# Norm statistics from sums and squares, a planner with measured step lengths, and two early gradient blocks in a forward-and-backward kernel of four layers

## The chip, the cores and the metric

The kernel runs on one NeuronCore of a Trainium2 chip. The metric is the time of one execution on the device in microseconds (us). Some executions of a program are slower as a whole. A profile is one execution taken with the hardware profiler. PE is TensorE (PEld its weight loads), DVE is VectorE, ACT is ScalarE, POOL is GpSimd. The granted clock is the share of PE's full clock that the profile shows as granted to it. An eviction is the copy of a matmul result out of PE's output memory.

## The reference

A residual stack of a linear-attention block A and a gated block B is applied twice (A, B, A, B; layers 0 to 3). Each block reads a layer norm without gain or bias. The kernel returns the result and all gradients.

```python
def _layernorm(x, axis=-1, eps=1e-5):
    m = jnp.mean(x, axis=axis, keepdims=True)
    v = jnp.var(x, axis=axis, keepdims=True)
    return (x - m) / jnp.sqrt(v + eps)
# x is (1, 2048, 512) bf16; A: 32 heads of 16; B: sigmoid(x @ w_gate) * (x @ w_up) @ w_down, width 1376
x = x + _A_ref(_layernorm(x), A_wqkv, A_wo)
x = x + _B_ref(_layernorm(x), B_w_gate, B_w_up, B_w_down)
x = x + _A_ref(_layernorm(x), A_wqkv, A_wo)
x = x + _B_ref(_layernorm(x), B_w_gate, B_w_up, B_w_down)
# outputs: x, and the gradients of A_x, A_wqkv, A_wo, w_gate, w_up, w_down for a given grad_out
```

## The kernel before

The tokens are worked in 8 blocks of 256, each in two halves of 128, in five sweeps over the blocks; the weight gradients end the program. The order of all instructions comes from a small planner in the kernel. Each piece of work states how long it holds PE (`pe`), which steps follow on other engines and how long each takes (`post`), and which buffers it takes and gives back. While the program is built, an event loop plays these pieces through. Whenever an engine is idle, the ready piece with the longest remaining path is emitted on it. The emitted order is then fixed: an engine runs its instructions in that order, whatever the real times are.

```python
class Plan:
    HOP = dict(PE=0.22, A=0.16, V=0.16, P=0.16, D=2.2)   # us from the end of a step to its follower
    SLACK = 1.3                                          # stretches the paths that set priorities
    RATE = 0.27                                          # MB per us of a DMA
    ...
EARLY = 1
PULL = (10.0, 10.0, 0.0)          # extra priority of some transposes
AHEAD2, AHEAD3 = (2, 0), (2, 0)   # how far attention may run ahead of the gated block
TURN = (0, 1, 1)                  # which blocks are transposed by PE and which by DMA
```

The norm of half a block takes its statistics on DVE:

```python
nc.vector.bn_stats(stats[:], x_t[:, j, :])
nc.vector.bn_aggr(mv[:], stats[:])
nc.gpsimd.tensor_scalar(rs, mv[:, 1:2], EPS_LN, None, ALU.add)
nc.gpsimd.tensor_tensor(rs, rs, k.neghalf[:, 0:1], ALU.pow)
nc.vector.scalar_tensor_tensor(nmr[:], mv[:, 0:1], -1.0, rs, ALU.mult, ALU.mult)
nc.scalar.activation(h[:, j, :], x_t[:, j, :], ACT.Identity, bias=nmr[:], scale=rs)
...
# in a_p2, the residual add of a linear-attention block:
nc.vector.tensor_tensor(k.x[l, b][:, j, :], ps[:], st["xin"][:, j, :], ALU.add)
```

In the last gated layer, `EARLY` says for how many blocks the product of the output gradient with the transposed down weights (`dhh`) is made ahead, as pieces of its own. It depends only on inputs, so it can fill holes.

Of the kernel before, what the change touches and what calls it, by code (L numbers as in the profile page):

```python
# [17 lines left out]
D = 512  # L18
# [56 lines left out]
class Plan:  # L75
# [8 lines left out]
    HOP = dict(PE=0.22, A=0.16, V=0.16, P=0.16, D=2.2)  # L84
    SLACK = 1.3
# [5 lines left out]
    def add(self, key, fn, pe=0.0, deps=(), post=(), use="", side=False, pull=0.0):  # L91
        u = Piece(len(self.pieces), key, fn, pe, list(deps), [(p + ("",))[:3] for p in post], marks(use), side, pull)
        u.post = [(e, c, marks(m)) for e, c, m in u.post]
        assert key not in self.by_key, key
        self.pieces.append(u)
        self.by_key[key] = u
# [168 lines left out]
PHI = [("A", 0.5, "+s1"), ("V", 0.2), ("V", 0.62, "-s1 -mm")]  # L265
EARLY = 1
PULL = (10.0, 10.0, 0.0)
AHEAD2, AHEAD3 = (2, 0), (2, 0)
TURN = (0, 1, 1)
# [126 lines left out]
def build_consts(k, consts):  # L396
    nc = k.nc
    k.consts = consts
    k.ident = consts.tile([P, P], BF16, name="ident")
    nc.gpsimd.memset(k.ident[:], 0.0)  # L400
    nc.gpsimd.affine_select(out=k.ident[:], in_=k.ident[:], compare_op=ALU.not_equal, fill=1.0,
                            base=0, pattern=[[-1, P]], channel_multiplier=1)
    k.neghalf = consts.tile([P, 2], F32, name="neghalf")
    nc.gpsimd.memset(k.neghalf[:], -0.5)
    k.ones_col = consts.tile([P, 1], BF16, name="ones_col")
    nc.gpsimd.memset(k.ones_col[:], 1.0)
    k.bdmask = consts.tile([P, P], BF16, name="bdmask")
    nc.gpsimd.memset(k.bdmask[:], 1.0)
    nc.gpsimd.affine_select(out=k.bdmask[:], in_=k.bdmask[:], compare_op=ALU.is_ge, fill=0.0,
                            base=0, pattern=[[-16, 8], [0, 16]], channel_multiplier=1)  # L410
    nc.gpsimd.affine_select(out=k.bdmask[:], in_=k.bdmask[:], compare_op=ALU.is_ge, fill=0.0,
                            base=15, pattern=[[16, 8], [0, 16]], channel_multiplier=-1)

    k.hs = consts.tile([P, NDC, P], BF16, name="hs")
    nc.gpsimd.memset(k.hs[:], 0.0)
    for o in (0, H):
        v = k.hs[:, :, o:o + H]
        nc.gpsimd.memset(v, 1.0)
        nc.gpsimd.affine_select(out=v, in_=v, compare_op=ALU.is_ge, fill=0.0,
                                base=0, pattern=[[128, NDC], [-16, H]], channel_multiplier=1)  # L420
        nc.gpsimd.affine_select(out=v, in_=v, compare_op=ALU.is_ge, fill=0.0,
                                base=15, pattern=[[-128, NDC], [16, H]], channel_multiplier=-1)
    k.spread = consts.tile([P, NDC, P], BF16, name="spread")
    k.rr = [consts.tile([P, 2, P], BF16, name=f"rr{i}") for i in range(2)]
    for r in k.rr:
        nc.gpsimd.memset(r[:], 0.0)
    k.rr_i = 0
    k.rstd = [consts.tile([P, 2 * NBLK], F32, name=f"rstd{l}") for l in range(4)]
    k.rstdh = {l: consts.tile([P, 2 * NBLK], F32, name=f"rstdh{l}") for l in (1, 3)}
# [25 lines left out]
def add_turn(k, key, get, put, name, deps, pull=0.0):  # L455
# [8 lines left out]
    for j in range(2):  # L464
        k.G.add(f"{key}.{j}", lambda j=j: half(j), NDC * C128, deps[j] + ([f"<{key}.0"] if j else []), [("A", 0.52, "-tp")],
                "+tp" if j else "+tp +t2", pull=pull)
# [12 lines left out]
def layernorm(k, l, b, x_fn, deps):  # L479

    nc, G = k.nc, k.G

    def half(j):
# [19 lines left out]
        if l in k.rstdh:  # L503
            yield
            nc.gpsimd.tensor_scalar(k.rstdh[l][:, col], rs, 0.5, 0.0, ALU.mult, ALU.add)
    for j in range(2):
        G.add(f"LN{l}.{b}.{j}", lambda j=j: half(j), 0.0, deps[j] + ([f"LN{l}.{b}.0@s"] if j else []),
              [("V", 0.62, "+ln @s"), ("V", 0.07), ("P", 0.19), ("P", 0.63), ("V", 0.07), ("A", 0.7, "@h" if l in k.rstdh else "@h -ln")]
              + ([("P", 0.25, "-ln")] if l in k.rstdh else []), "" if j else "+t2")
# [16 lines left out]
def a_k(k, l, b, keep, by_dma=False):  # L526
# [69 lines left out]
    if l == 2 and b in SUMS:  # L596
        gs, prev = SUMS[b]
        for m in range(NDC):
            G.add(f"GS{n}.{m}", lambda m=m: gsum(m, gs, True, True), 2 * len(gs) * C512,
                  [f"K{l}.{bb}.{j}" for bb in gs for j in range(2)] + [f"GS{l}.{prev}.{m}"] + ([f"<GS{n}.{m - 1}"] if m else []),  # L600
                  [("A", 0.5, "-mm") if b == 1 else ("V", 0.62, "-mm")],
                  "+mm" + (" +accf" if b == 1 and m == 0 else " +w4" if b == NBLK - 1 and m == 0 else ""))
    if b % 2 == 1:
        bs = [b - 1, b]
        ks = [f"K{l}.{bb}.{j}" for bb in bs for j in range(2)]
        G.add(f"ZS{n}", zsum, 16 * 0.027, ks + [f"ZS{l}.{b - 2}", f"ZB{l - 2}"], [("V", 0.1, "-tp")], "+tp")
# [13 lines left out]
def cpost(i, tag):  # L620
    return [("A", 0.5, "-" + tag)] if i % 2 == 0 else [("V", 0.6, "-" + tag)]


def a_barrier(k, l):
# [42 lines left out]
    G.add(f"KV{l}", kv, 16 * C128, cg + ["WV", f"KT{l - 2}", f"WT{l - 2}.3", f"ZN{l - 2}"], [("V", 0.62, "-mm")], "+mm")  # L667
# [33 lines left out]
    for m in range(NDC):  # L701
        G.add(f"WT{l}.{m}", lambda m=m: wpt(m), 4 * C128, wps + ([f"<WT{l}.{m - 1}"] if m else []), [("A", 0.5, "-mm")],
              "+mm" if m else "+mm +w4")
    if l == 0:
        G.store("SW", lambda: nc.sync.dma_start(out=k.WpT_d[:], in_=flat(A.WpT[:])), 2 * BLK, [f"WT{l}.{m}" for m in range(NDC)], "-w4")
    G.add(f"ZB{l}", zbd, 0.0, [f"ZS{l}.{last}"] + wps, [("V", 0.7, "+s1"), ("V", 0.1)])
    G.add(f"ZN{l}", lambda: turn("Zn"), 4 * C128, [f"ZB{l}"], [("A", 0.5, "-tp")], "+tp -s1")
    G.add(f"KT{l}", lambda: turn("kv"), 4 * C128, wps, [("A", 0.5, "-tp")], "+tp")
# [32 lines left out]
def a_p2(k, l, b, xin_fn, deps, late):  # L741
# [54 lines left out]
    def y(j):  # L796
# [3 lines left out]
        for c in range(NDC):  # L800
            nc.tensor.matmul(ps[:], lhsT=A.pn[b][:, c, tslice(j)], rhs=A.Wp[:, c, :], start=(c == 0), stop=(c == NDC - 1))  # L801
        yield
        nc.vector.tensor_tensor(k.x[l, b][:, j, :], ps[:], st["xin"][:, j, :], ALU.add)
    G.load("LX" + n, lx, BLK if l == 0 else 2 * BLK, [f"YA{l}.{b - 2}.1", f"SX{l - 1}.{b}"] + deps, "+t2" if l == 0 else "+xb")
    G.add("DE" + n, den, 8 * 0.027, [f"Q{n}.0", f"Q{n}.1", f"ZZ{l}", f"<YA{l}.{b - 2}.1"],
          [("V", 0.15, "+dn -tp"), ("V", 0.5), ("V", 0.1, "+rr"), ("V", 0.12, "-dn")], "+tp")
    G.add("RT" + n, turn, 2 * C128, ["DE" + n, "SPREAD"] + late, [("V", 0.3, "-tp +rT")], "+tp -rr")
    for hf in range(2):
        G.add(f"SP{n}.{hf}", lambda hf=hf: spread(hf), 2 * C256, ["RT" + n] + ([f"<SP{n}.0"] if hf else []),
              [("V", 0.62, "@pn"), ("V", 0.2, "+s1"), ("V", 0.62, "-s1 -mm")], "+mm" if hf else "+mm +t2 +t2")  # L810
# [8 lines left out]
    for j in range(2):  # L819
        G.add(f"YA{n}.{j}", lambda j=j: y(j), 4 * C512, pn + ["LX" + n] + [f"WP{l}.{c}" for c in range(NDC)] + ([f"<YA{n}.0"] if j else []),  # L820
              [("V", 0.62, "-mm")], "+mm +xb" if j == 0 and l == 0 else "+mm")
# [4 lines left out]
def a_b1(k, l, b, deps):  # L826
# [56 lines left out]
    for j in range(2):  # L883
        G.add(f"CA{n}.{j}", lambda j=j: cast(j), 0.0, [f"LB{lx}.{b}.{j}", "LN_" + n, f"<MS{l}.{b - 2 if b % 2 else b - 3}.3"]
              + ([f"CA{n}.0"] if j else []), [("A", 0.52)], "" if j else "+t2")
    add_turn(k, f"TG{n}", lambda: st["g"], lambda t: st.__setitem__("gT", t), f"gT{l}", [[f"CA{n}.{j}"] for j in range(2)])
    for hf in range(2):
        G.add(f"DP{n}.{hf}", lambda hf=hf: dpn(hf), 8 * C256,
              [f"TG{n}.0", f"TG{n}.1"] + ([f"LP{n}", "WPL0"] if l == 0 else [f"LP{n}"]) + ([f"<DP{n}.0"] if hf else [f"<DP{l}.{b - 1}.1"]) + [f"WT{l}.{m}" for m in range(NDC)],
              [("V", 0.45), ("V", 0.45)], "+mm +s1" if hf else "+mm +s1 +t2")  # L890
        G.add(f"ZE{n}.{hf}", lambda hf=hf: zn(hf), 2 * C256, [f"DP{n}.{hf}", f"ZN{l}"] + ([f"<ZE{n}.0"] if hf else [f"<ZE{l}.{b - 1}.1"]),
              [("V", 0.45), ("V", 0.45, "-s1"), ("V", 0.6, "-mm")], "+s1 -s1")
# [3 lines left out]
    if b in SUMS:  # L896
# [20 lines left out]
        for m in range(NDC):  # L917
# [3 lines left out]
                  [("A", 0.5, "-mm") if b == 1 else ("V", 0.62, "-mm")],  # L921
# [4 lines left out]
def a_bbarrier(k, l):  # L926
# [61 lines left out]
    G.add(f"DT{l}", dkvT, 16 * C128, ms + ["WOT"], [("V", 0.62, "-mm")], "+mm +s1")  # L988
# [3 lines left out]
    G.add(f"DZ{l}", dz, 0.0, [f"ZE{l}.{b}.{hf}" for b in range(NBLK) for hf in range(2)], [("V", 0.12)] * 5)  # L992
# [3 lines left out]
    G.add(f"DKV{l}", dkv, 16 * C128, [f"<U{l}.3"] + ms, [("V", 0.62, "-mm")], "+mm")  # L996
# [23 lines left out]
def add_lnb(k, l, b, fn, deps, ps_tag, more=""):  # L1020

    for j in range(2):
        k.G.add(f"LB{l}.{b}.{j}", lambda j=j: ln_bwd(k, l, b, j, *fn(j)), 0.0, deps[j] + ([f"LB{l}.{b}.0@s"] if j else []),
                [("A", 0.7, "@s +lnf +s1 -" + ps_tag), ("V", 0.66, "-s1"), ("P", 0.3), ("V", 0.62), ("V", 0.65, "-lnf")],
# [3 lines left out]
def a_b2(k, l, b, x_load, out, deps, out_use=""):  # L1028
# [51 lines left out]
    for hf in range(2):  # L1080
        G.add(f"DK{n}.{hf}", lambda hf=hf: half(hf), 8 * C256, ["LDH" + n, "LDP" + n, f"DZ{l}"] + ([f"<DK{n}.0"] if hf else [f"<DK{l}.{b - 1}.1"]) + [f"U{l}.{m}" for m in range(NDC)],
              [("V", 0.2, "+s1"), ("V", 0.4), ("V", 0.4, "-s1 -mm")], "+mm" if hf else "+mm +t2")
# [11 lines left out]


# [30 lines left out]
def glu_fwd(k, l, b):  # L1126
# [28 lines left out]
    def y(p):  # L1155
# [6 lines left out]
        if p == NPAIR - 1:  # L1162
            for j in range(2):
                yield
                nc.vector.scalar_tensor_tensor(x[0, b][:, j, :], st["acc"][j][:], 0.5, x[0, b][:, j, :], ALU.mult, ALU.add)
    for p in range(NPAIR):
# [3 lines left out]
              [("A", 0.46, "+th -mm"), ("V", 0.58, "-mm @hh"), ("P", 0.55), ("V", 0.58, "-th")],  # L1170
              "+mm +mm" if p else "+mm +mm +hh +w11")
        G.add(f"Y{n}.{p}", lambda p=p: y(p), q * 2 * C512, [f"G{n}.{p}@hh", "WD"] + ([f"<Y{n}.{p - 1}"] if p else []),
              [("V", 0.62, "-acc @0"), ("V", 0.62, "-acc")] if p == NPAIR - 1 else [], "" if p else "+acc +acc")
# [37 lines left out]
def glu_both(k, l, b):  # L1211
# [58 lines left out]
    if early:  # L1270
        for p in range(NPAIR):
            G.add(f"E{n}.{p}", lambda p=p: dhh_early(p), len(pair_chunks(p)) * 4 * C256,
                  ["LG" + n, "WWD"] + ([f"<E{n}.{p - 1}"] if p else [f"<E{l}.{b - 1}.5"]), [("A", 0.46, "-mm")],
# [4 lines left out]
    for p in range(NPAIR):  # L1278
        q = len(pair_chunks(p))
        ops = [("A", 0.46, "+th -mm"), ("A", 0.46, "+s1 +s1 +pr -mm"), ("V", 0.58, "-mm @hh"), ("V", 0.58, "@u"), ("V", 0.58, "-th"), ("V", 0.35, "-s1 -s1")]  # L1280
        mm = "+mm +mm +mm"
        if early:
            ops = [ops[0], ("V", 0.58, "+s1 +pr -mm @hh")] + ops[3:5] + [("V", 0.35, "-s1")]
# [3 lines left out]
              ops, mm if p else mm + " +hh")  # L1287
# [23 lines left out]
    for j in range(2):  # L1311
        G.add(f"Y3{n}.{j}", lambda j=j: part(j), 11 * C512, [f"G{n}.{p}@hh" for p in range(NPAIR)] + ([f"<Y3{n}.0"] if j else []),
              [("V", 0.62, "-mm")], "+mm" if j else "+mm +t2")
# [6 lines left out]
def glu_bwd(k, l, b):  # L1320
# [43 lines left out]
    for j in range(2):  # L1364
        G.add(f"CB{n}.{j}", lambda j=j: cast(j), 0.0, [f"LB2.{b}.{j}"] + ([f"CB{n}.0"] if j else []), [("A", 0.52)],
              "" if j else "+th" if b < 2 else "+hh" if b in (2, 4) else "+t2" if b > 5 else "")
    add_turn(k, "TB" + n, lambda: k.g1[b], lambda t: st.__setitem__("gT", t), "gT1", [[f"CB{n}.{j}", f"<G1{l}.{b - 1}.1"] for j in range(2)], PULL[2])
    for p in range(NPAIR):
# [3 lines left out]
              [("A", 0.46, "+s1 +pr -mm"), ("V", 0.35, "@u"), ("V", 0.35, "-s1")], "+mm")  # L1372
# [85 lines left out]
def sweep2(k):  # L1458
# [10 lines left out]
    for b in range(NBLK):  # L1469
        a_p2(k, 0, b, lambda b=b: xin(b), [f"LN2.{b - 3}.1@h", f"<G1.{b - AHEAD2[0]}.0"], [f"<G1.{b - AHEAD2[0]}.{AHEAD2[1]}"])  # L1470
        layernorm(k, 1, b, lambda b=b: k.x[0, b], [[f"YA0.{b}.{j}"] for j in range(2)])
# [7 lines left out]
        layernorm(k, 2, b, lambda b=b: k.x[0, b], [[f"Y1.{b}.5@0", f"<GS2.{2 * (b // 2) - 3}.3"], [f"Y1.{b}.5"]])  # L1479
        G.free("-xb", [f"LN2.{b}.{j}" for j in range(2)] + [f"SX1.{b}"])  # L1480
        a_k(k, 2, b, b < 2, TURN[0] <= b < last)
# [5 lines left out]
def sweep3(k):  # L1487
# [19 lines left out]
    for b in range(NBLK):  # L1507
        a_p2(k, 2, b, lambda b=b: xin(b), [f"<Y33.{b - 3}.1", f"<G3.{b - AHEAD3[0]}.0"], [f"<G3.{b - AHEAD3[0]}.{AHEAD3[1]}"])
        layernorm(k, 3, b, lambda b=b: k.x[2, b], [[f"YA2.{b}.{j}"] for j in range(2)])
# [67 lines left out]
def dw(k):  # L1577
# [60 lines left out]
    def epost(i):  # L1638
        return [("A" if i % 2 == 0 else "V", 0.6, "+s1 -mm")]
# [94 lines left out]
    mid = [f"<J{ng[0] - 4}.3"]  # L1734
    for m in range(NDC):
        G.add(f"JV.{m}", lambda m=m: dwv(m), 8 * C128, ["FG0", "FG2", "DKV0", "DKV2"] + mid, epost(m), "+mm")
        G.store(f"SV.{m}", lambda m=m: nc.sync.dma_start(out=k.outs["wqkv"][cslice(m), 2 * D:3 * D], in_=st["v", m][:]), BLK / 2, [f"JV.{m}"], "-s1")
        G.add(f"JO.{m}", lambda m=m: dwo(m), 2 * C512, ["FM0", "FM2"] + mid, epost(m + 1), "+mm")
# [31 lines left out]
```

## Time and profile before

The median was 1141.45 us in three runs (1141.18 to 1143.3).

The page of the profile of the kernel before: the span, then busy time, share of the span and number of instructions by engine.

```profile
span 1137.5 us, 20073 instructions
PE 1089.5 (96%) x7652; PEld 711.2 (63%) x7652; DVE 694.7 (61%) x1711; ACT 337.5 (30%) x639; POOL 119.9 (11%) x295
```

PE is the bound. Since no matmul can be dropped, what is to be won is PE's idle time, 1137.5 − 1089.5 = 48.0 us, and a little more where PE runs at a lower clock. The next view shows where the idle time is. These are windows of the same execution: the window and its length, then busy time and instruction count of PE, PEld, DVE, ACT and POOL, and at the end the granted PE clock, the share of the DMA engines and GB/s.

```profile
0.00:50.00 50.00, 41.34 (x313) 23.95 (x314) 34.39 (x98) 34.58 (x57) 16.77 (x52) 1.00 0.78 250
50.00:90.00 40.00, 33.18 (x291) 24.75 (x290) 35.42 (x90) 17.14 (x29) 7.84 (x18) 0.96 0.35 109
...
205.00:290.00 85.00, 74.23 (x616) 50.57 (x614) 71.48 (x161) 31.90 (x55) 12.22 (x29) 1.00 0.83 197
290.00:520.00 230.00, 227.95 (x1632) 154.68 (x1630) 180.50 (x422) 81.23 (x154) 20.94 (x49) 1.00 0.70 180
520.00:610.00 90.00, 84.10 (x553) 51.02 (x552) 66.79 (x181) 27.15 (x56) 2.29 (x9) 0.98 0.81 230
...
740.00:870.00 130.00, 121.26 (x720) 67.77 (x718) 94.48 (x258) 29.52 (x66) 4.74 (x20) 0.99 1.03 246
870.00:1140.00 270.00, 262.75 (x1839) 178.43 (x1836) 19.05 (x35) 15.06 (x32) 0.00 (x0) 1.00 0.89 195
```

The length less PE's busy time is PE's idle time: 8.7, 6.8, 10.8, 2.0, 5.9 and 8.7 us, and to the end of the span 4.8 us (267.5 − 262.75). The holes lie where one sweep gives way to the next (50-90, 205-290, 520-610, 740-870) and at both ends. In between PE is full, even in 90-205, where DVE is 91% busy (104.57 of 115 us).

What PE waited for, longest in total first (engine and tile, releaser, total us, times, longest), whole execution:

```profile
PE hTk_ps L450 <- ACT h L502: 7.0, 1, 7.0
PE ya_ps L801 <- DVE rphiT L794: 3.6, 3, 2.3
PE dpn_ps L857 <- DVE dqT L880: 2.9, 2, 2.5
PE q_ps L726 <- DMA hTq<-h_d: 2.3, 1, 2.3
```

The first is the start of the program. The rest are many small waits, none over 2.5 us.

The statistics on DVE, as groups of instructions (line, engine, operation, tiles, shapes, count, then busy us and mean ns of one, then idle time of the engine before them):

```profile
L492 DVE BATCH_NORM_STATS2 ln_stats<-xa 128x6 f32<-128x512 f32 x32 | 21.5, 671 | 0.0
L494 DVE BATCH_NORM_AGGREGATE ln_mv<-ln_stats 128x2 f32<-128x6 f32 x64 | 11.0, 172 | 0.3
L500 DVE SCALAR_TENSOR_TENSOR ln_nmr<-ln_mv,rstd 128x1 f32<-128x1 f32 x64 | 11.0, 172 | 4.1 <-POOL rstd L498 3.9
```

### The profile page before, as it was taken

To read this page: it belongs to the slowest core of one execution; us is meant where nothing else is said; L and a number is where in the kernel's file an instruction comes from. 1 tells how busy PE (TensorE), PEld (TensorE's weight loads), DVE (VectorE), ACT (ScalarE), POOL (GpSimd) and SP (SyncE) were. 2 spreads that over 40 slices of the span, in tenths; PEclk is the share of its full clock that TensorE was granted. 3 is DMA by queue.
4 is the path that set the end of the run, shared out by engine and by line. 5 is a ranking of instruction groups with operands and counts; after the bars stand their busy time and mean duration, and the time that the engine had idled before them with its cause. 6 is when DMAs were issued, how large, how long until landed. Compare 5 with 4: busy or idle time off the path is not lost.

```text
span 1137.5 us, 20073 instructions
## 1 busy us (share of the span) xinstructions
PE 1089.5 (96%) x7652; PEld 711.2 (63%) x7652; DVE 694.7 (61%) x1711; ACT 337.5 (30%) x639; POOL 119.9 (11%) x295
## 2 busy tenths in 40 slices
PE   7979999978999999999899999997999999999998
PEld 4657666646566676676555665654544456666787
DVE  6789989779867987778956577678754000000001
ACT  7642444334333333234144444431211000000001
POOL 4123435201201000100000000000000000000000
PEclk9999999999999999999999999999999999999999
DMA  7737898994777767755979979979999999999852
GB/s 240 244 93 242 237 297 227 262 217 131 199 192 187 185 172 190 189 164 150 249 206 284 252 216 270 271 188 255 283 250 261 245 229 234 201 281 216 148 115 70
DMA packets 491392, 242.97 MB, mean 214 GB/s; under 512 B 297280, under 2 KB 475680, under 8 KB 489248
## 3 DMA queue, kind: packets, MB, share of 16 engines
q1 hardware_dynamic: 491296, 241.69, 83.0%
q8 instruction: 60, 0.98, 0.4%
q14 instruction: 36, 0.29, 0.1%
HBM read 68.75 MB, written 100.43 MB: 149 GB/s over the span
## 4 chain that ended last, share of the span: by engine, by line
PE 86%; DVE 6%; DMA 3%; ACT 2%; issue 2%; SPq 1%; POOL 0%; DVEq 0%; ACTq 0%
PE dw_ps L1652 25%; PE dha_ps L1072 7%; PE dh_acc L1186 7%; PE dh_acc L1188 7%; PE dhh_ps L1119 6%; PE g_ps L1119 6%; PE u_ps L1119 6%; PE y_ps L1307 3%; PE y_acc L1160 3%; PE dpk_ps L1056 2%; PE ya_ps L801 2%; PE k_ps L537 2%; PE dpn_ps L857 2%; PE m_ps L906 2%; PE g_ps L563 2%
## 5 line engine op out<-in xcount | busy, mean ns | idle before, releaser
L1652 PE MATMUL dw_ps<-dw_set,h 128*128 128x352 bf16 (+2 forms) x1536 | 205.6, 297 | 0.0
L1652 PEld LDWEIGHTS <-h 128*128 128x128 bf16 x1536 | 150.3, 98 | 55.1
L1635 DVE TENSOR_SCALAR dw_o<-dw_ps 128x512 bf16<-128x512 f32 (+3 forms) x33 | 17.8, 541 | 246.6 <-PE dw_ps L1652 242.0
L1186 PE MATMUL dh_acc<-wuT,du 128*128 128x512 bf16 x352 | 133.4, 379 | 1.2 <-ACT lnb_t L1007 1.2
L1188 PE MATMUL dh_acc<-wgT,dg 128*128 128x512 bf16 x352 | 133.4, 379 | 0.2 <-DVE dg L1361 0.2
L1633 ACT ACTIVATE dw_o<-dw_ps 128x512 bf16<-128x512 f32 (+4 forms) x34 | 16.3, 481 | 264.7 <-PE dw_ps L1652 249.2
L1119 PE MATMUL g_ps<-hT,wg 128*128 128x256 bf16 x704 | 92.5, 272 | 0.1
L1119 PE MATMUL u_ps<-hT,wu 128*128 128x256 bf16 x704 | 92.5, 273 | 0.0
L1119 PE MATMUL dhh_ps<-gT,wdT 128*128 128x256 bf16 x704 | 89.7, 273 | 1.1 <-ACT dhh L1268 0.7
L1119 PEld LDWEIGHTS <-wg 128*128 128x128 bf16 x704 | 68.2, 98 | 20.4 <-issue 0.4
L1652 PE MATMUL dw_ps<-g,dw_set 128*128 128x512 bf16 (+1 forms) x352 | 78.4, 384 | 1.6 <-DVE dqT L880 1.6
L1119 PEld LDWEIGHTS <-wdT 128*128 128x128 bf16 x704 | 68.7, 98 | 15.7 <-issue 1.8
L1119 PEld LDWEIGHTS <-wu 128*128 128x128 bf16 x704 | 68.9, 98 | 8.0
L1013 POOL TENSOR_SCALAR ab<-c 128x2 f32<-128x2 f32 x64 | 18.8, 294 | 505.3 <-DVE lnb_j L1010 505.2
L1652 PEld LDWEIGHTS <-dw_set 128*128 128x128 bf16 (+1 forms) x352 | 35.5, 101 | 42.7 <-issue 3.7
L1188 PEld LDWEIGHTS <-dg 128*128 128x128 bf16 x352 | 34.4, 98 | 35.4 <-issue 1.5
L1186 PEld LDWEIGHTS <-du 128*128 128x128 bf16 x352 | 34.4, 98 | 33.1
L1241 ACT ACTIVATE th<-g_ps 128x512 f32<-128x512 f32 (+1 forms) x48 | 26.9, 559 | 91.5 <-PE g_ps L1119 63.5
L1007 ACT ACTIVATE lnb_t<-dha_ps,rstd 128x512 f32<-128x512 f32 x32 | 22.0, 687 | 88.3 <-PE dha_ps L1072 59.6
L1160 PE MATMUL y_acc<-wd,hh 128*128 128x512 bf16 x176 | 43.2, 379 | 0.0
L1359 DVE TENSOR_TENSOR du<-s2tl,dhh 128x512 bf16<-128x512 bf16 (+1 forms) x48 | 19.0, 400 | 39.3 <-ACT dhh L1354 36.4
L1144 ACT ACTIVATE th<-g_ps 128x512 f32<-128x512 f32 (+1 forms) x48 | 26.8, 557 | 54.6 <-PE g_ps L1119 32.8
(187 smaller groups left out, 1833.0 us busy)
## 6 DMA issues: line engine op xcount, KB each, us to landing
s2t_d<-s2t SPq DMA_DIRECT2D x8, 1408.0 KB, 6.8
s2tl<-s2t_d SPq DMA_DIRECT2D x8, 1408.0 KB, 8.1
hh_d<-hh SPq DMA_DIRECT2D x16, 640.0 KB, 4.5
du_d<-du SPq DMA_DIRECT2D x80, 128.0 KB, 2.8
dg_d<-dg SPq DMA_DIRECT2D x80, 128.0 KB, 2.7
h_d<-h SPq DMA_DIRECT2D x32, 256.0 KB, 2.7
h<-h_d SPq DMA_DIRECT2D x18, 256.0 KB, 4.5
pk_d<-pk SPq DMA_DIRECT2D x16, 256.0 KB, 3.1
```

The lines of the kernel that those rows point to most:

```text
L537: nc.tensor.matmul(ps[:], lhsT=A.hT[b][:, m, tslice(j)], rhs=k.wk[:, m, :], start=(m == 0), stop=(m == NDC - 1))
L563: nc.tensor.matmul(ps[:], lhsT=k.h[l, bb][:, j, cslice(m)], rhs=A.pk[bb][:, j, :], start=(first and i == 0), stop=(last and i == len(its) ...
L801: nc.tensor.matmul(ps[:], lhsT=A.pn[b][:, c, tslice(j)], rhs=A.Wp[:, c, :], start=(c == 0), stop=(c == NDC - 1))
L1072: nc.tensor.matmul(ps[:], lhsT=lh[:, c, tslice(j)], rhs=rh[:, c, :], start=(i + c == 0), stop=(i == 2 and c == NDC - 1))
L1119: nc.tensor.matmul(ps[:, i, :], lhsT=w[:, m, fsl(fc)], rhs=rhsT[:, m, :], start=(m == 0), stop=(m == NDC - 1))
L1144: nc.scalar.activation(th[:, 0:w], flat(gp[:])[:, 0:w], ACT.Tanh, scale=0.5)
L1160: nc.tensor.matmul(st["acc"][j][:], lhsT=st["hh"][:, fc, tslice(j)], rhs=k.wd[:, fc, :], start=(fc == 0), stop=(fc == NFC - 1))
L1186: nc.tensor.matmul(acc[j][:], lhsT=du[:, i, tslice(j)], rhs=k.wuT[:, fc, :], start=(fc == 0), stop=False)
L1188: nc.tensor.matmul(acc[j][:], lhsT=dg[:, i, tslice(j)], rhs=k.wgT[:, fc, :], start=False, stop=(fc == NFC - 1))
L1241: nc.scalar.activation(th[:, 0:w], flat(gp[:])[:, 0:w], ACT.Tanh, scale=0.5)
L1307: nc.tensor.matmul(ps[:], lhsT=st["hh"][:, fc, tslice(j)], rhs=k.wd[:, fc, :], start=(fc == 0), stop=(fc == NFC - 1))
L1652: nc.tensor.matmul(ps, lhsT=lhs(s_), rhs=rhs(s_), start=(s_ == 0), stop=(s_ == 31))
```

## The change

Its intent has three parts. First, 46 of the 64 norm halves take their statistics off DVE: the residual adds also sum their result, ACT sums the squares, and POOL does the small arithmetic. Second, the planner gets the step lengths that the trace shows, a `LAP` of 0.08 us by which a step overlaps the one before it on its engine, and a slack of 1. Third, two blocks instead of one make `dhh` early. With these go new settings and freer placement of the last small weight gradients (`JV`, `JO`). The diff, cut to its core (`...` marks cuts):

```diff
-    HOP = dict(PE=0.22, A=0.16, V=0.16, P=0.16, D=2.2)
-    SLACK = 1.3
+    HOP = dict(PE=0.25, A=0.14, V=0.14, P=0.14, D=2.2)
+    LAP = 0.08
+    SLACK = 1.0
...
-        u.post = [(e, c, marks(m)) for e, c, m in u.post]
+        u.post = [(e, c if e == "D" else c - self.LAP, marks(m)) for e, c, m in u.post]
...
-PHI = [("A", 0.5, "+s1"), ("V", 0.2), ("V", 0.62, "-s1 -mm")]
-EARLY = 1
-PULL = (10.0, 10.0, 0.0)
-AHEAD2, AHEAD3 = (2, 0), (2, 0)
-TURN = (0, 1, 1)
+PHI = [("A", 0.6, "+s1"), ("V", 0.29), ("V", 0.69, "-s1 -mm")]
+EARLY = 2
+SUMMED = (0, 7, 0)     # layer 1: blocks from 0; layer 2: blocks below 7; layer 3: blocks from 0
+PULL = (10.0, 10.0, 10.0)
+AHEAD2, AHEAD3 = (2, 3), (2, 0)
+TURN = (6, 1, 1)
...
+    def half_sums(j):
...
+        nc.scalar.activation(h[:, j, :], x_t[:, j, :], ACT.Square, accum_out=q[:, 0:1])
+        nc.gpsimd.tensor_tensor(q[:, 1:3], sx.to_broadcast([P, 2]), k.pm[:], ALU.mult)
+        nc.gpsimd.tensor_scalar(q[:, 0:1], q[:, 0:1], 1.0 / D, EPS_LN, ALU.mult, ALU.add)
+        nc.gpsimd.tensor_scalar(rs, q[:, 1:2], q[:, 2:3], q[:, 0:1], ALU.mult, ALU.add)
+        nc.gpsimd.tensor_tensor(rs, rs, k.neghalf[:, 0:1], ALU.pow)
+        nc.gpsimd.tensor_tensor(q[:, 3:4], q[:, 1:2], rs, ALU.mult)
+        nc.scalar.activation(h[:, j, :], x_t[:, j, :], ACT.Identity, bias=q[:, 3:4], scale=rs)
...
-        nc.vector.tensor_tensor(k.x[l, b][:, j, :], ps[:], st["xin"][:, j, :], ALU.add)
+        nc.vector.scalar_tensor_tensor(k.x[l, b][:, j, :], ps[:], 1.0, st["xin"][:, j, :], ALU.mult, ALU.add,
+                                       accum_out=k.sx[l + 1][:, 2 * b + j:2 * b + j + 1])
... (the same accum_out on the other residual add; some forty step lengths replaced)
-    mid = [f"<J{ng[0] - 4}.3"]
-        G.add(f"JV.{m}", lambda m=m: dwv(m), 8 * C128, ["FG0", "FG2", "DKV0", "DKV2"] + mid, epost(m), "+mm")
+        G.add(f"JV.{m}", lambda m=m: dwv(m), 8 * C128, ["FG0", "FG2", "DKV0", "DKV2"], epost(m), "+mm", pull=40.0)
```

## The prediction

> **What bounds the kernel now.** TensorE. The page gives PE 1089.5 us busy of a 1137.5 us span (96%); DVE 61%, ACT 30%, POOL 11%. The chain of waits is 86% PE. In the PE timeline back-to-back matmuls start 109 ns (256 columns) or 216 ns (512 columns) apart, so a busy PE is at its pace. Only PE idle time, about 48 us, can be won. Windows of 25 us place it: 0-25 has 7.8 us idle (7.0 of it before the first transpose), 50-75 6.3, 225-275 10.8, 300-325 1.5, 525-575 5.5, 750-800 7.3, 825-850 1.4, and about 5 us of tail, mostly the last store. 100-225 and 870-1130 are full. In 50-75, 525-550 and 775-800 the granted clock is 0.93: each loses some 1.7 us more. The Trainium skill ("TensorE: Matmul & The Clock Gate", Part 1) says an idle window of about 3.4 us halves the clock; the trace agrees that the clock falls only where the PE waits.
>
> **What the change removes, adds, moves.** No matmul goes, one more block (8 transposes, 0.4 us) is added.
> - DVE: 46 normalisation halves lose BN_STATS (671 ns), BN_AGGREGATE (172) and the -mean*rstd op (172): about 47 us. The adds that now also sum cost perhaps 0.05-0.1 us each, 48 of them: +3 us. Net about -43 us, 30 of it in 55-250.
> - ACT: 46 x (a square pass of about 0.69 plus a 0.2 accumulator read, the durations of the lnb_t pair) = +41 us.
> - POOL: four more 0.29 us scalar steps, less one, per half: +40 us. POOL has room, but the chain of one half becomes longer: 2.7 us before, about 3.5 after, without queueing.
> - Two early blocks instead of one: 4.8 us of dhh matmuls become free to fill the start of the third sweep, and one block is turned by PE, not DMA.
> - Schedule from measured step lengths. The gradient pieces of V and O move off the last microseconds.
>
> **How much is critical.** DVE is 92-98% busy in 100-200, but PE is full there, so relief there buys nothing at once. It helps at the edges, where PE waits name DVE:
> - 50-75 (waits on rphiT 3.6 us, pqT 1.7 us): I expect 2.5-3 us back plus part of the cold clock.
> - 225-275 (pk, z, Zn, h, the hTq load 2.3): 4-5 us, of which most by the second early block.
> - 525-575 and 750-850 have the same work on DVE; 1-2 us by better ordering.
> - 300-325 and tail: 1 us.
> DMA waits (hTq 2.3 us, hT 1.4, first load) stay.
> Sum: about 11 us.
>
> **Predicted: 1130 us, 8 in 10 between 1118 and 1140.** Faster by over 2% (below 1118.6): 0.10. Within 2%: 0.87. Slower by over 2%: 0.03.
>
> **What would show it.** PE busy within 3 us of 1089; PE idle down from 48 to about 37. Windows: idle in 50-75 near 3.5, in 225-275 near 6, in 750-800 still over 5. DVE busy about 650, ACT about 380, POOL about 160. Granted clock in 50-75 above 0.93. DVE share in 100-200 falls to 80%, PE there unchanged.
>
> **What would make it wrong.** The square leaving the table set of exp and tanh: more than the one ACT_TABLE_LOAD (1.28 us) of now ("ScalarE: Activation LUTs", Table sets, says a set holds a fixed group; no run here shows square in it). The longer POOL chain delaying the transposed blocks at the start of a sweep. The new order colliding with DMA, which is at 1.0 share in 200-250. Or a much better order at the two backward transitions, which I have not credited: that could win 8 us more.

## More of the kernel before

The transposed weights `wuT` and `wgT` are loaded by DMA, and a small memset on POOL then clears padding rows. The planner does not count this memset as a step.

## The result, and the profile after

The changed kernel took 1131.49 us (median of 4, 1127.41 to 1133.16), against 1142.38 us (4 runs, 1141.18 to 1144.55) for the kernel before. The ratio is 0.9897, with a 95% interval of 0.9865 to 0.9929. A ratio in this document is the mean time of one kernel's fast runs over that of the other's of the same rounds, so it is not quite the ratio of the medians quoted. Later the same changed kernel was run again as a control (label c0_after_again), on a chip where the kernel before took 1138.58 us: 1131.24 us, ratio 0.9932 (0.9919 to 0.9945). So the gain is 7 to 11 us, under one per cent to about one. The two ratios of one and the same kernel differ by 0.0035, which is 4 us: differences of that size between rounds say little.

The page of the changed kernel, and the engine line of the control:

```profile
span 1131.4 us, 20151 instructions
PE 1083.4 (96%) x7559; PEld 710.9 (63%) x7660; DVE 663.1 (59%) x1621; ACT 365.6 (32%) x733; POOL 156.1 (14%) x435
```

```profile
PE 1090.0 (96%) x7660; PEld 710.8 (63%) x7660; DVE 662.9 (59%) x1621; ACT 365.9 (32%) x733; POOL 156.8 (14%) x435
```

The first trace holds only 7559 matmul records for 7660 weight loads, so its PE busy time is too small. The control has all 7660, and PE's idle time is read from it: its span was 1130.6 us, so 1130.6 − 1090.0 = 40.6 us were idle, 7.4 less than before. The windows of the control:

```profile
0.00:50.00 50.00, 40.03 (x292) 22.19 (x293) 33.48 (x93) 33.37 (x55) 16.70 (x54) 1.00 0.79 247
50.00:90.00 40.00, 36.03 (x307) 26.28 (x305) 35.65 (x91) 17.74 (x35) 11.43 (x33) 0.96 0.35 105
...
205.00:290.00 85.00, 78.90 (x617) 51.82 (x616) 64.61 (x147) 39.11 (x76) 21.98 (x57) 0.98 0.86 211
290.00:520.00 230.00, 227.63 (x1650) 155.77 (x1648) 175.98 (x402) 87.17 (x175) 28.79 (x74) 1.00 0.71 180
520.00:610.00 90.00, 82.22 (x548) 49.29 (x547) 64.68 (x180) 28.25 (x59) 2.92 (x10) 1.00 0.80 221
...
740.00:870.00 130.00, 123.00 (x722) 68.28 (x721) 92.05 (x242) 28.09 (x63) 5.56 (x20) 0.99 1.05 251
870.00:1140.00 270.00, 257.67 (x1815) 176.14 (x1813) 17.41 (x33) 14.96 (x32) 0.00 (x0) 1.00 0.87 189
```

PE's idle time by stretch (its length, the last one cut at the end of the span, less PE busy); the last column is a kernel that comes up later:

| stretch, us | before | changed (control) | c1_searched |
|---|---|---|---|
| 0-50 | 8.7 | 10.0 | 9.7 |
| 50-90 | 6.8 | 4.0 | 4.1 |
| 90-205 | 0.3 | 0.0 | 0.0 |
| 205-290 | 10.8 | 6.1 | 1.4 |
| 290-520 | 2.0 | 2.4 | 2.1 |
| 520-610 | 5.9 | 7.8 | 3.7 |
| 610-740 | 0.0 | 0.5 | 0.0 |
| 740-870 | 8.7 | 7.0 | 7.1 |
| 870-end | 4.8 | 2.9 | 2.9 |
| all | 48.0 | 40.6 | 31.0 |

Three holes shrank (50-90, 205-290, the end) and one a little (740-870); two grew (0-50, 520-610). The longest waits of PE in the control read the same way: small, and still naming DVE and ACT.

```profile
PE hTk_ps L456 <- ACT h L532: 6.9, 1, 6.9
PE hTk_ps L456 <- ACT hTk L458: 4.0, 4, 2.0
PE ya_ps L833 <- DVE rphiT L826: 3.9, 2, 2.0
```

The groups of the changed kernel that replaced the statistics, and the only table load of ACT:

```profile
L496 ACT ACTIVATE h<-xa 128x512 bf16<-128x512 f32 x30 | 18.8, 626 | 25.5 <-DVE xa L835 19.4 <-DVE xa L1203 5.8
L496 ACT ACTIVATION_READ_ACCUMULATOR h<-xa 128x1 f32 x30 | 5.7, 189 | 0.0
L532 ACT ACT_TABLE_LOAD x1 | 1.3, 1283 | 3.7 <-DMA x<-in_A_x_dram 3.7
L835 DVE DVE_READ_ACCUMULATOR x2l<-ya_ps,x2l 128x1 f32 x16 | 1.4, 86 | 0.0
L502 POOL TENSOR_SCALAR rstd<-ln_q 128x1 f32<-128x1 f32 x46 | 21.4, 465 | 3.4
```

The summing add costs no more than the add (679 to 688 ns before and after); its sum is read out by an instruction of its own of 82 to 86 ns. The square takes 626 ns and its read-out 189 ns.

The end of the program also changed. The last pieces of the chain of waits of the kernel before (start, us, what), then of the changed kernel:

```profile
1130.94 2.81 DMA out_dram<-dw_o
1133.87 0.69 DVE dw_o L1635
```

```profile
1092.72 35.82 PE dw_ps L1691 x328
1128.61 0.38 ACT dw_o L1672
```

Before, the last pieces were eight short ones in a row (`JV`, `JO`), and the last eviction waited until a store had given an output buffer free. After, the end is one ordinary group and its eviction. That is the step from 4.8 to 2.9 us in the table.

### The profile page after: what moved, and what is told of

It is laid out like the page before. It is cut to its first block, busy times and chain, and to the rows that moved or that the text cites. A ratio compares the mean times of both kernels' runs of the same rounds, so it can differ in the third digit from the quotient of the medians.

```text
span 1131.4 us, 20151 instructions
## 1 busy us (share of the span) xinstructions
PE 1083.4 (96%) x7559; PEld 710.9 (63%) x7660; DVE 663.1 (59%) x1621; ACT 365.6 (32%) x733; POOL 156.1 (14%) x435
## 4 chain that ended last, share of the span: by engine, by line
PE 85%; DVE 6%; SPq 2%; ACT 2%; issue 2%; DMA 1%; POOL 1%; DVEq 0%; ACTq 0%
PE dw_ps L1691 24%; PE dha_ps L1105 7%; PE dh_acc L1227 7%; PE g_ps L1157 6%; PE u_ps L1157 6%; PE dhh_ps L1157 6%; PE dh_acc L1225 6%; PE y_ps L1346 3%; PE y_acc L1198 3%; PE q_ps L758 2%; PE dpk_ps L1089 2%; PE ya_ps L833 2%; PE k_ps L569 2%; PE m_ps L939 2%; PE g_ps L595 1%
## 5 line engine op out<-in xcount | busy, mean ns | idle before, releaser
L1225 PE MATMUL dh_acc<-wuT,du 128*128 128x512 bf16 x323 | 122.5, 379 | 0.3
L1280 ACT ACTIVATE th<-g_ps 128x512 f32<-128x512 f32 (+1 forms) x48 | 26.8, 558 | 55.3 <-PE g_ps L1157 42.1
L1187 DVE SCALAR_TENSOR_TENSOR hh<-th,u_ps 128x512 bf16<-128x512 f32 (+1 forms) x48 | 30.8, 641 | 18.5 <-ACT th L1182 11.4
```

The costliest lines, as they stand in the source:

```text
L1187: nc.vector.scalar_tensor_tensor(hh, th[:, 0:w], 1.0, flat(up[:])[:, 0:w], ALU.add, ALU.mult)
L1225: nc.tensor.matmul(acc[j][:], lhsT=du[:, i, tslice(j)], rhs=k.wuT[:, fc, :], start=(fc == 0), stop=False)
L1280: nc.scalar.activation(th[:, 0:w], flat(gp[:])[:, 0:w], ACT.Tanh, scale=0.5)
```

## The experiments

The question was which part gives the gain. Theories:

- **Edges**: the relief of DVE and the second early block fill the holes at the sweep starts. This is the prediction's reason.
- **Order**: the true step lengths, by themselves, make a better order.
- **Luck**: any new order moves the time by some us, up or down.
- **Planner** (formed after the first four runs): the settings had been chosen so that the planner's own end time is low. What moves that end time moves the time on the chip, and no part has a value of its own.

The planner's end time is called *planned* below. It is what the event loop in the kernel works out while the program is built. It is not a measurement. It is 1139.2 us for the kernel before (with its old lengths) and 1124.1 us for the changed one. All kernels here gave correct results. The first four kernels ran beside the kernel before at a median of 1138.73 us, the next four at 1138.58 us, the last four at 1138.92 us; each of these rounds was on another chip, so ratios are compared across them, not times.

### First: the change less one part

`a1_no_sums`: all statistics back on DVE.

```diff
-SUMMED = (0, 7, 0)
+SUMMED = (8, 0, 8)
... (and the two residual adds without accum_out)
```

> The changed kernel with the norm statistics put back on VectorE (all 64 halves by BN_STATS, the residual adds without sums); everything else of the change kept. Edges theory (relief of VectorE and the early block fill the two sweep starts): 3 to 5 us slower than the changed kernel, ratio to the kernel before about 0.993, the loss in 50-90 us; 205-290 us keeps its gain. Order theory (the step lengths make the better order): within 1.5 us of the changed kernel, ratio 0.989 to 0.991. Luck theory (any new order moves the time by some us, up or down): change of either sign, in stages that the statistics do not touch as well.

Measured: 1142.29 us, ratio 1.0028 (1.0009 to 1.0047). That is 0.0096, or 11 us, worse than the control's ratio: more than the whole gain of the change. PE idle in 50-90 rose to 6.2 us, as expected. But the loss is not there alone: in 205-290 PE idled *less* (3.7 us) than in the changed kernel.

`a2_one_early`: one early block.

```diff
-EARLY = 2
+EARLY = 1
```

> The changed kernel with one early gradient block instead of two. Edges theory: 3 to 4 us slower than the changed kernel, ratio about 0.993, with the lost PE time of 205-290 us back from 8.7 to about 12.5 us and 50-90 us still near 5.7. Order theory: within 1.5 us of the changed kernel. Luck theory: either sign, elsewhere too.

Measured: 1136.28 us, ratio 0.9967 (0.9948 to 0.9986), 4 us worse than the control. The size fits the edges theory. The place does not. These are the windows 205-290 and 290-520 of the changed kernel's first trace and then of this one (both traces lack 100 or 101 matmul records, so they can be compared with each other):

```profile
205.00:290.00 85.00, 77.53 (x604) 51.58 (x612) 64.31 (x146) 38.77 (x75) 21.88 (x57) 0.98 0.85 210
290.00:520.00 230.00, 226.00 (x1621) 155.78 (x1648) 176.05 (x402) 87.12 (x175) 28.73 (x74) 1.00 0.71 180
```

```profile
205.00:290.00 85.00, 78.96 (x615) 52.62 (x623) 65.39 (x150) 38.95 (x77) 21.81 (x57) 0.98 0.84 217
290.00:520.00 230.00, 220.16 (x1580) 151.70 (x1605) 173.65 (x408) 86.60 (x173) 25.55 (x74) 1.00 0.67 174
```

Without the second early block PE is busier in 205-290 (78.96 against 77.53 us) and idler in 290-520 (9.8 against 4.0 us). So the second block did not fill the hole at the start of the third sweep. One reason can be read from the traces: of the second block's 44 `dhh` matmuls the changed kernel placed few there. It ran 60 `dhh` matmuls in 205-290 (the kernel before 44, this one 52), and 16 more at 0.109 us are 1.7 us. The loss came later: most of it lies in 440-480, where PE idled 6.1 us here and 0.3 us in the changed kernel. Whether the missing block or the new order did that is not shown.

`a3_old_steps`: the old step lengths, hops and slack; everything else as changed.

```diff
-    HOP = dict(PE=0.25, A=0.14, V=0.14, P=0.14, D=2.2)
-    LAP = 0.08
-    SLACK = 1.0
+    HOP = dict(PE=0.22, A=0.16, V=0.16, P=0.16, D=2.2)
+    SLACK = 1.3
... (all step lengths as before)
```

> The changed kernel ordered with the old step lengths (old hops, no overlap term, slack 1.3, old costs); statistics, early blocks, turns and ends as in the change. Edges theory: within 2 us of the changed kernel, ratio 0.988 to 0.992. Order theory: 5 us or more slower, ratio 0.995 to 1.0, the loss spread over all sweep changes. Luck theory: either sign, a few us.

Measured: 1153.91 us, ratio 1.0126 (1.0103 to 1.0150), 22 us worse than the control. This favours the order theory, or luck.

`a4_old_knobs`: the old settings and the old end.

```diff
-PULL = (10.0, 10.0, 10.0)
-AHEAD2, AHEAD3 = (2, 3), (2, 0)
-TURN = (6, 1, 1)
+PULL = (10.0, 10.0, 0.0)
+AHEAD2, AHEAD3 = (2, 0), (2, 0)
+TURN = (7, 1, 1)
... (JV and JO at the very end, as before)
```

> The changed kernel with the old hand settings (turn by PE only for the last block of the third layer's keys, no pull on the turns of the first gated layer's gradient, old look-ahead) and the V and O weight-gradient pieces back at the very end. Edges theory: about 2 us slower from the end (5.2 us from the last matmul to the end of the span instead of 3.1) and about 1 us from the turn; ratio about 0.992. Order theory: within 1.5 us. Luck theory: either sign.

Measured: 1135.45 us, ratio 0.9967 (0.9947 to 0.9988), 4 us worse than the control.

What follows: taking any one of four parts away costs 11, 4, 22 and 4 us, together 41 us, out of a gain of 7 to 11. The parts do not add up: what one is worth depends on the others and on the settings. (The two losses of 4 us are no larger than the difference between the two rounds of the changed kernel.) The planned times of these four kernels were 1138.8, 1132.6, 1142.6 and 1131.9 us. Three of them ended 3.5 to 3.7 us over plan. That gave the planner theory, which the next runs test.

### Second: does the planned time tell the time?

`c0_after_again`: the control, unaltered.

> The changed kernel itself, unaltered, beside the others on one chip: the control. The four kernels undone in part ended 3.5, 3.7, 11.3 and 3.5 us later than the planner in the kernel had worked out for them (1138.8, 1132.6, 1142.6, 1131.9 us); the three with 3.5 to 3.7 use the new step lengths. If the planner is true to a constant with the new lengths, this one (planned 1124.1) ends at 1127 to 1129 where the kernel before ends at 1138.7. Edges theory says only that the ratio is 0.990 as before.

Measured: 1131.24 us, ratio 0.9932, 7.1 us over plan. The expectation (1127 to 1129) was missed by 2 us: the plan is not true to a constant.

`c1_searched`: the settings come from search over the planned time; planned 1119.9 us.

```diff
-SUMMED = (0, 7, 0)
-PULL = (10.0, 10.0, 10.0)
-AHEAD2, AHEAD3 = (2, 3), (2, 0)
+SUMMED = (0, 0, 0)
+PULL = (60.0, 5.0, 30.0)
+AHEAD2, AHEAD3 = (2, 2), (2, 4)
```

> The changed kernel with hand settings that a search over the planner's own time found: statistics by sums in layers 2 and 4 only, other pulls, other look-ahead, two early blocks; planned 1119.9 us, 4.2 us under the changed kernel. Planner theory (the new lengths make the planned time true to a constant, so whatever lowers the planned time lowers the time): 4 us faster than the control, ratio about 0.986. Edges theory: no faster than the control, since it does less of the relief (layer 3 stays on VectorE), rather 1 to 3 us slower. Luck theory (planned times do not carry over to the chip): anywhere from 3 us faster to 8 us slower.

Measured: 1117.92 us, ratio 0.9808 (0.9790 to 0.9826). This is 13 us faster than the control, although layer 2 of its norms is back on DVE. (The expectations count layers from 1: their layers 2, 3 and 4 are layers 1, 2 and 3 here.) It beats both kernels; whether by 2% over the kernel before is unclear. The direction fits the planner theory; the size (13 us for 4 planned) does not. Its windows 50-90, 205-290 and 520-610, and its engine line:

```profile
50.00:90.00 40.00, 35.93 (x322) 27.09 (x319) 37.87 (x97) 19.52 (x39) 15.34 (x43) 1.00 0.44 133
205.00:290.00 85.00, 83.64 (x682) 56.61 (x680) 69.17 (x164) 38.88 (x73) 17.76 (x48) 1.00 0.85 206
520.00:610.00 90.00, 86.27 (x566) 51.20 (x565) 64.01 (x162) 32.03 (x68) 4.31 (x12) 1.00 0.93 246
PE 1084.6 (97%) x7660; PEld 710.1 (64%) x7660; DVE 672.2 (60%) x1663; ACT 358.5 (32%) x705; POOL 140.1 (13%) x393
```

Of the 15.0 us between the two spans (1130.6 and 1115.6), 9.6 are idle time (40.6 against 31.0). The other 5.4 are busy time of the same 7660 matmuls (1090.0 against 1084.6). Part of that is the clock, granted 1.00 in 50-90 and 205-290 where the control had 0.96 and 0.98. Over the whole span the grant was 0.998 against 0.995, which is an estimated 0.003 × 1130 = 3.4 us. The remaining 2 us are not explained.

`c2_none_searched`: neither sums nor a second early block, but the new lengths and searched settings; planned 1129.7 us.

```diff
-EARLY = 2
-SUMMED = (0, 7, 0)
-PULL = (10.0, 10.0, 10.0)
-AHEAD2, AHEAD3 = (2, 3), (2, 0)
-TURN = (6, 1, 1)
+EARLY = 1
+SUMMED = (8, 0, 8)
+PULL = (5.0, 0.0, 5.0)
+AHEAD2, AHEAD3 = (2, 1), (3, 5)
+TURN = (6, 1, 2)
... (and the two residual adds without accum_out)
```

> Neither of the two named parts: all norm statistics on VectorE, one early block, the new step lengths, V and O pieces as in the change, and hand settings found by the same search under these bounds; planned 1129.7 us. Planner theory: 5.5 us slower than the control, ratio about 0.995, so nearly half of the gain without either part. Edges theory: no gain at all or worse, ratio 1.0 or more (the run without sums alone gave 1.003). Luck theory: above 1.0 by some us.

Measured: 1139.13 us, ratio 0.9991 (0.9974 to 1.0007), 9.4 us over plan. Lengths and settings without the two parts gained nothing measurable here. The planner theory's size (0.995) was a miss; the edges theory's 1.0 held.

`b2_steps_only`: the kernel before with nothing but the new lengths (those of the diff under a3_old_steps, the other way).

```diff
-HOP = dict(PE=0.22, A=0.16, V=0.16, P=0.16, D=2.2)
-SLACK = 1.3
+HOP = dict(PE=0.25, A=0.14, V=0.14, P=0.14, D=2.2)
+LAP = 0.08
+SLACK = 1.0
... (and all step lengths)
```

> The kernel before with the new step lengths and nothing else: same statistics, one early block, old hand settings. Planned 1151.7 us. Planner theory: 1155 us where the kernel before ends at 1138.7, ratio 1.014: truer lengths alone make it slower, because the old settings had been chosen for the old lengths. Order theory of the first round (the lengths by themselves make a better order): faster than before, ratio 0.99 to 0.995. Luck theory: within some us of before.

Measured: 1152.80 us, ratio 1.0120 (1.0104 to 1.0136), 1.1 us over plan. Truer lengths alone made it 14 us slower. The order theory falls as it was put: the lengths by themselves do not make a better order.

### Third: single settings, and the search with false lengths

`d1_no_third_sums`: the changed kernel with one setting altered.

```diff
-SUMMED = (0, 7, 0)
+SUMMED = (0, 0, 0)
```

> The changed kernel with one setting altered: the third layer's statistics go back to VectorE (14 of 46 halves); layers 2 and 4 keep the sums. Planned 1120.8 us, 3.3 under the changed kernel. Planner theory: 3 to 10 us faster than the changed kernel (ratio 0.993 in the last round), so ratio 0.984 to 0.990. Edges theory (more relief of VectorE is better): slower by 1 to 3 us, ratio 0.994 to 0.996.

Measured: 1125.52 us, ratio 0.9877 (0.9861 to 0.9893), 0.0055 or 6 us better than the control. Fewer sums, faster: with these settings, the order that the planner made with relief in layer 2 was the worse one. PE idle in 205-290 fell from 6.1 to 2.1 us (85 − 82.95):

```profile
205.00:290.00 85.00, 82.95 (x668) 56.09 (x666) 67.54 (x162) 38.91 (x73) 18.82 (x49) 0.98 0.85 208
```

The trace shows one reason. POOL in the control around 215 us, in order of time (start, us, engine, line, operation, tiles, and in brackets the idle time before and what ended it), then ACT of the same stretch:

```profile
210.66 0.62 POOL L1189 TENSOR_SCALAR s2t<-th 128x512 bf16<-128x512 f32 x1 [0.57 <-ACT th L1182]
220.39 0.52 POOL L1464 MEMSET wuT<- 32x512 bf16 x1 [9.11 <-DMA wuT<-in_B_w_up_dram]
220.88 0.18 POOL L498 TENSOR_TENSOR ln_q<-sx,pm 128x2 f32<-128x2 f32 x1
```

```profile
215.27 0.19 ACT L496 ACTIVATION_READ_ACCUMULATOR h<-xa 128x1 f32 x1
223.01 0.81 ACT L508 ACTIVATE h<-xa,ln_q,rstd 128x512 bf16<-128x512 f32 x1 [4.89 <-POOL ln_q L506]
```

The sum of squares was read out by 215.5 us. POOL took it up at 220.88 us, because the padding memset of `wuT` stood before it in POOL's queue, and that memset waited for the weights' DMA. The Trainium skill ("TensorE: Matmul & The Clock Gate", the specification table's row on queue depth) gives GpSimdE a strict first-in-first-out queue; this trace agrees: POOL was idle for 9.11 us before the memset, and during the last 5 us of that the step behind it was ready. The norm was done at 223.82 us, and PE's transposes of it and the keys came late. In d1 the same norm (POOL from 214.84, ACT `h` at 216.02) goes ahead of the memset, which there runs only at 232.73 us (2 of the 7 us between the two `h` were won earlier: the residual add began at 211.96 instead of 214.00 us):

```profile
214.84 0.22 POOL L526 TENSOR_SCALAR rstd<-ln_mv 128x1 f32<-128x1 f32 x1 [4.20 <-DVE ln_mv L524]
232.73 0.51 POOL L1464 MEMSET wuT<- 32x512 bf16 x1 [8.81 <-DMA wuT<-in_B_w_up_dram]
```

The planner cannot see this, since the memset is no step of its model. That the blocked step was late is shown. How much of the 6 us it explains is not: the whole order differs between the two kernels, the planner, which knows nothing of the memset, had itself planned 3.3 us less for this one, and a kernel with only the memset moved was not run.

`c3_one_early_searched`: sums, one early block, settings searched under that bound; planned 1122.1 us.

```diff
-EARLY = 2
-SUMMED = (0, 7, 0)
-PULL = (10.0, 10.0, 10.0)
-AHEAD2, AHEAD3 = (2, 3), (2, 0)
+EARLY = 1
+SUMMED = (0, 4, 1)
+PULL = (60.0, 10.0, 5.0)
+AHEAD2, AHEAD3 = (2, 3), (2, 0)
```

> Sums and one early block only, with settings that the search found under that bound; planned 1122.1 us, 2.2 more than the searched kernel with two early blocks (ratio 0.981) and 7.6 less than the searched one without sums and with one early block (ratio 0.999). Planner theory: ratio 0.983 to 0.988, so the second early block is worth 2 to 7 us and the sums 10 us or more. Edges theory: about 0.985 to 0.990 for the same reason. If it ends near 0.999, the second early block carries the gain, not the sums.

Measured: 1127.88 us, ratio 0.9899 (0.9883 to 0.9916). Against c2_none_searched (0.9991), which had the same search but no sums, this is 0.0092, about 10 us, better; the plans differ by 7.6 us. Against c1_searched (0.9808) it is 10 us worse, where the plans differ by 2.2 us. So after a search the sums and the second early block each go with a gain of up to 10 us. How far these are values of the parts is open: one kernel of each kind was run, and kernels stray from their plans by 3.2 us (see below), so a difference of two is uncertain by an estimated 1.4 × 3.2 = 4.5 us.

`e1_old_searched`: all parts, but the old, false lengths, and settings that the same search found on their planned time; planned 1120.3 us.

```diff
... (lengths, hops and slack as in a3_old_steps)
-SUMMED = (0, 7, 0)
-PULL = (10.0, 10.0, 10.0)
-AHEAD2, AHEAD3 = (2, 3), (2, 0)
-TURN = (6, 1, 1)
+SUMMED = (1, 1, 2)
+PULL = (10.0, 0.0, 5.0)
+AHEAD2, AHEAD3 = (2, 2), (2, 1)
+TURN = (6, 3, 1)
```

> All parts of the change, but ordered with the old step lengths, with settings that the same search found on the planned time of the old lengths: planned 1120.3 us, as low as the searched kernel with the new lengths (planned 1119.9, ratio 0.981). If the truth of the lengths matters: 8 to 20 us slower than that one, ratio 0.988 to 1.0 (the changed kernel with old lengths ended 11.3 us over its plan). If only the search matters and any lengths would do: ratio 0.979 to 0.984.

Measured: 1122.91 us, ratio 0.9859 (0.9835 to 0.9884). It fell between the two expectations, below what was put down for "the truth of the lengths matters". With false lengths, a searched order beat the changed kernel by 0.0073, about 8 us, and lost to c1_searched, the one with true lengths, by 0.0051, about 6 us. Under the false lengths the search gained 0.0267, about 30 us (a3_old_steps had 1.0126). So here the search mattered more than the truth of the lengths.

`f1_deep_searched`: true lengths, a longer search that may also shift single priorities; planned 1114.6 us.

```diff
-    SLACK = 1.0
+    SLACK = 1.1
-            u.prio = prio[u.key]
+            u.prio = prio[u.key] + 0.5 * ((u.n * 2654435761 + 61010 * 40503) % 4093 / 4093.0)
-SUMMED = (0, 7, 0)
-PULL = (10.0, 10.0, 10.0)
-AHEAD2, AHEAD3 = (2, 3), (2, 0)
+SUMMED = (0, 3, 0)
+PULL = (5.0, 10.0, 5.0)
+AHEAD2, AHEAD3 = (2, 2), (2, 1)
```

> The changed kernel with settings from a longer search that may also shift each piece's priority by up to 0.5 us by a fixed pattern, and the slack; planned 1114.6 us, 5.4 under the searched kernel of the last round (1117.9 us measured). Planner theory: 1110 to 1118 us, ratio 0.975 to 0.982. Luck theory: at or above 0.985.

Measured: 1120.44 us, ratio 0.9835 (0.9820 to 0.9850). It beats the changed kernel, but not c1_searched, although its plan was 5.3 us lower.

### What the plans were worth

| kernel | lengths | planned | measured | over plan |
|---|---|---|---|---|
| b2_steps_only | new | 1151.7 | 1152.8 | 1.1 |
| a1_no_sums | new | 1138.8 | 1142.3 | 3.5 |
| a2_one_early | new | 1132.6 | 1136.3 | 3.7 |
| a4_old_knobs | new | 1131.9 | 1135.5 | 3.6 |
| c2_none_searched | new | 1129.7 | 1139.1 | 9.4 |
| c0_after_again | new | 1124.1 | 1131.2 | 7.1 |
| c3_one_early_searched | new | 1122.1 | 1127.9 | 5.8 |
| d1_no_third_sums | new | 1120.8 | 1125.5 | 4.7 |
| c1_searched | new | 1119.9 | 1117.9 | −2.0 |
| f1_deep_searched | new | 1114.6 | 1120.4 | 5.8 |
| kernel before | old | 1139.2 | 1138.7 | −0.5 |
| e1_old_searched | old | 1120.3 | 1122.9 | 2.6 |
| a3_old_steps | old | 1142.6 | 1153.9 | 11.3 |

With the new lengths the time is the plan plus 4.3 us, with a standard deviation of 3.2 us over these ten. Among these ten, every plan that was over 5.3 us lower was the faster kernel; three pairs with plans 2.2 to 5.3 us apart came out the other way round. Three old-length kernels scatter from −0.5 to 11.3 us, too few to say more. How rugged the ground is shows in the plan alone: 800 random draws of these settings, with the new lengths, gave planned times with a median of 1144.1 us and 5% to 95% limits of 1131.6 and 1160.7 us. Two of the 800 were as low as the changed kernel's 1124.1.

What stands of the theories: the planner theory holds roughly, to some 5 us. Its second half, that no part has a value of its own, is not shown: against the kernel before, new lengths and searched settings without the two parts gained nothing (c2), with the sums 12 us (c3), with both 22 us (c1). The edges theory holds in 50-90: with the new lengths and all sums of layer 1, PE idled 4.0 to 4.1 us there in the five kernels with complete traces (control, d1, c1, c3, f1), and with no sums 5.6 us in both (b2, c2). Luck is not excluded for any difference of under some 5 us.

## Why the prediction was right or wrong

The time was right: 1130 us predicted, 1131.49 us measured, within the range of 1118 to 1140 us, and "within 2%" came true. Point by point:

- **The bound.** Right. PE's busy time stayed (1089.5 and, in the control, 1090.0 us), and what moved is idle time: 48.0 to 40.6 us, against "about 37" predicted.
- **Relief of DVE in 90-205 buys nothing at once.** Right. DVE in 100-200 fell to 80%, as predicted (80.2 of 100 us), and PE was full before and after.
- **DVE −43 us.** Oversized: 694.7 to 663.1, so −31.6 us. The step that failed is the term "about 47 us". It multiplied 46 by the durations of the three steps, but short steps overlap on DVE. In the trace of before a step of 172 ns was followed 0.09 us after its start, so 46 × (0.60 + 0.09 + 0.09) = 36 us is the better estimate, less 48 read-outs of 84 ns.
- **ACT about 380, POOL about 160.** ACT came to 365.6 for the same reason of overlap and a square of 626 ns rather than 690. POOL came to 156.1.
- **50-75: 2.5 to 3 us.** Right in size (2.8 us in 50-90), and the sums are a fitting cause: without them (a1, b2, c2) 5.6 to 6.2 us are idle there. "Part of the cold clock" was wrong: the grant in 50-75 stayed at 0.93 in the changed kernel.
- **205-290: 4 to 5 us, "of which most by the second early block".** Right in size (10.8 to 6.1), wrong in cause. This is the step that failed. Only 16 more `dhh` matmuls, 1.7 us, ran in the window than before, and without that block (a2) the hole is no larger; what a2 lost it lost in 290-520. With other settings the step could have come true: c1_searched ran all 88 `dhh` matmuls of its two blocks there, and 1.4 us stayed idle. But c3_one_early_searched, with one block, also had only 3.4 us. What filled 205-290 cannot be put down to one part: with the old lengths alone 9.5 us were idle there, with the old settings 8.2 us, and with fewer sums 2.1 us. (The traces of a1, a3 and a4 each lack about 100 of some 7,660 matmul records, so their idle figures may be too high, by an estimated 1.4 us in this window: that is how far the two traces of the changed kernel differ in it, 78.90 against 77.53 us.)
- **525-575 and 750-850: 1 to 2 us by better ordering.** Wrong for the first (520-610 grew from 5.9 to 7.8), right for the second (740-870 fell by 1.7).
- **The end: 1 us with 300-325.** The end alone gave 1.8 us, and with the old end put back (a4) 4.8 us were idle there again.
- **The risk of a second table set.** It did not come: one table load, as before. The Trainium skill ("ScalarE: Activation LUTs", Table sets) says that a table set holds a fixed group of functions; the square ran in this kernel beside exp and tanh without a further load.
- **"The longer POOL chain delaying the transposed blocks at the start of a sweep."** Named as a risk, and it happened, if not by the length of the chain: the POOL queue held a norm back by 5 us behind a memset.

So the time came out right, with one cause misplaced and some luck. The gain was predicted as 11 us: it was 11 in the first round and 7 in the control. PE's idle time fell by 7.4 us: the four holes that shrank gave 11.1 us, as much as predicted, but 0-50 and 520-610 lost 1.3 and 1.9 us, which was not foreseen. The prediction also assumed that the parts have values that add. The runs showed that they do not: leaving out one part cost up to 22 us, and a change of one setting gained 6.

## What to carry to other kernels

When a planner fixes the order of instructions, a code change and its settings are one thing: judge a part only after the settings have been searched anew with and without it. Search the planner's own time, but send the best few to the chip, because here plans within about 6 us did not rank. Give the planner every instruction that waits in an in-order queue, even a small memset, since it can hold back ready work behind a DMA, by 5 us here (a planner that counts it was not tried).

## What the Trainium skill lacked or had wrong

- "TensorE: Matmul & The Clock Gate" (Part 1 and the closing table) advises no PE gap over about 3 us to keep the clock. Here shorter gaps did not always keep it. In the control PE waited 1.94 us until 59.50 us, and the grant was 0.50 from 60.2 to 63.6 us; it waited 2.00 us until 226.95 us, and the grant was 0.50 from 227.4 to 230.9 us. In c1_searched two gaps of 1.94 and 2.06 us in 50-75 left the grant at 1.00. What decides between the two is not shown. The grant also differs from run to run of one kernel: the changed kernel took 1127.41 us at a mean grant of 0.998 and 1130.71 to 1133.16 us at 0.994 or 0.995; but c3_one_early_searched took 1127.9 us at 0.995 and at 0.998.
- "ScalarE: Activation LUTs" (Table sets) does not say which sets hold the square. Here it ran with exp and tanh on a single table load (1283 ns). The page names the accumulator output without a cost; its read-out was an instruction of 189 ns.
- "VectorE: DVE Perf Modes" (Two Vector instructions with no wait between them) says that an accumulator output is a second instruction, without its length: 82 to 86 ns here, and the add before it was no longer for it.
- "GPSIMD Engine Reference" gives no cost for a one-column step. Here a scalar step of 128x1 with two operations took 239 ns with constants and 465 ns with both scalars read from memory; a product of two columns took 234 ns.
